# Local attention scores on 168 instead of 192 columns, with a new order of all engines

## The chip, the cores and the metric

The kernel runs on one core of a Trainium2 chip. The metric is the device time of one execution in microseconds (us); lower is better. Three runs of the kernel before took 410.26, 410.98 and 411.16 us, so the median is 410.98 us.

## The reference

The reference is a local-global attention followed by a gated MLP with spatial mixing. All inputs are float32. There are 4 batches, 8 heads, 768 positions and a head dimension of 64. Eight keys (`n_global`) are visible to every query, and a query sees the 96 positions up to its own (`n_local`).

```python
scores = scale * np.matmul(q, k.transpose(0, 1, 3, 2))
is_global = pos[None, :] < int(n_global)
is_local = (rel >= 0) & (rel < int(n_local))
keep = is_global | is_local
dist = np.where(is_global & ~is_local, float(n_local), np.abs(rel))
scores = np.where(keep, scores - slopes * dist, -1e9)
a = softmax(scores)
x = np.matmul(a, v)                       # heads side by side: 768 x 512 per batch
h = gelu(x @ w_in); u, v = halves of h    # 512 columns each
v_n = (v - mean) / sqrt(var + 1e-6) * g_ln
v_s = w_sg @ v_n + b_sg                   # over the 768 positions
out = x + (u * v_s) @ w_out
```

## The kernel before

The attention works in 48 units. A unit is one batch, one pair of heads (four pairs) and one of three thirds of the sequence, that is 256 queries in two tiles of 128 (`units`, line 984 and after). The unit with `u == 0` has the first tile of the sequence, whose 128 queries see only the tile's own 128 keys; every other tile is worked on in halves of 64 queries (`HQ`).

**Key columns of a half.** For 64 queries, `W` = 192 score columns are computed: 96 keys shared by both halves of the tile, and a second block of 96 that differs. `NG` = 32 places at the head of each second block hold the first 32 keys of the sequence, as places for global keys, and 64 hold local keys (`tile_keys`, `unit_keys`, `window`). A unit's keys and its 256 queries come as one load, `qk` (`load_qk`, L1073).

**A unit's steps.** `score` (L1102) issues 8 products of 64 x 64 weights in the four quarters of TensorE's array. In the trace each product is two loads of weights and two matmuls, so a unit shows 16 of each. `softmax` then runs per tile and head, four times per unit: VectorE adds the bias to the scores, scales and takes the row's extreme in one instruction (L1124, which a second record, the read of the accumulator, follows); ScalarE takes the exponential with the row sum (L1129); after one reciprocal per unit, GpSimd (L1149), ScalarE or VectorE multiplies by it. The result `p` is 128 x 2 x 192, taken as three 128 x 128 blocks and transposed. For the first 16 units TensorE transposes (L1210, copied to `pt` at L1215 or L1216). For the other 32, VectorE transposes blocks of 32 x 32 (L1178), four DMAs bring them to DRAM (`far`, L1186) and one brings them back as `pt` (L1190). `weigh` (L1237) then multiplies by `v` in quarters; from unit 20 on, two units go together.

**The MLP.** Its products split every float32 operand into a high and a low part and use three matmuls for each (L589, L590, L591; for the last batch's seven-product scheme L837). They fill TensorE between the attention's products, while batch b + 1's attention runs beside batch b's MLP. GpSimd and VectorE share the splits (L625, L759, L940).

**The order of the work.** The kernel builds a list of operations and a planner (`Plan.order`) places them on PE, ACT, DVE, POOL and the DMA queue of SP, by costs written into the file, by the places of each buffer kind (`PLACES`), and by a due time for each operation that is shifted by a number from the string `SHIFTS`, two characters per operation. Each engine's instructions are emitted in the planned order. Where the planner sees a long idle time of TensorE in the first 29 us it emits products of zeros (L538).

```python
SHIFTS = ( ... )           # two characters per operation: the shift of its due time
NG = 32
W = P + HQ                 # 192
NS = P - NG                # 96
KW = 6 * NS                # 576 key columns of a unit's load
```

`find_general` (L1476 and after) sends the kernel to a slow general path if `n_global` is above `NG` or `n_local` above 97.

Of the kernel before, what the change touches and what calls it, by code (L numbers as in the profile page):

```python
# [19 lines left out]
P = 128  # L20
# [8 lines left out]
NG = 32  # L29
# [7 lines left out]
W = P + HQ  # L37
NS = P - NG
KW = 6 * NS
# [12 lines left out]
    "U5NqP9XReIUIO2NiTdTqScajVZRSS7WOSISDSvSuX5RhRpLyXIPtXbTIUCUWMGTyMkYsTRT3dZU8PLX8SgX8RuXjTlUjUIZrUyUa"  # L52
    "QBNEVEUCaoV0TfOfNOVMUdMTP4KWhrUSUXSmUHScPlTRY0TPW3SkSCSjSeQGQhLJSmQTaeRMPqRRXCS5UFT6VVSTN7SLSPSsObTa"
    "PuV8Q2M7SpPRUnQzT9SVUDVaTcSlVWR0bMURVcUCNkVNWBWlUlPqPaXVQXRtQ5VSUAS5TWQqS4T2NhPsU0ZpRaRbQJNEROOYVoVB"
    "URMtU2UgWDRFSWRDPLRoUCTiTmSXMsV7SuRfVZOxayScT5TwX5PSPxPAc7UrUJT1cZHSOsUWX2W5QOTVY8UJVJUORISfPrX5WaV3"
    "SGNuSKYgNcP9RJJYVWPAVcSiX1STOWT0UCgoj2ajYER0RmXaS8VpOUVJUAUQO0OnaPSdbkJzLfWKLAQmWOUqSSQtQ2QLelQjU5WP"
    "VnMdd5R4QCXMQrWzO7WaMiRuGfOFrNPzWFGWRMVRRaErcvXuRxbEPZK5OsWlazP5deQlbwLcSyVkfLRaOkXCS0S3cVRagNMuZ5ck"
    "XeZfV1coWPVguuQ7U6W3S1NdU2HjWgWmRSLnLFRDPJU9RBPsVlULWgQrUqQqPJShP0KOYMKDjzXMdrJrT0YQMXWoTHSOcYSWNaFZ"
    "SfQzSjQ5WdSOZVRxQ6NrWXRXaEOySUIdQif4OZEVLvYLI47eXbRiSuSqckTpcNVBUAkbTeNDT9Y2VuTQTgUFWLYjRkZfUUTpUMQ1"
    "PLQ2XbSUOhM589UaembHVtWXUoMyUobgaaQnJCTDUWSUN6WoV2UNM8aXXEPKRgFATsQvJDQRWeXTTIOOe6YkDSNDZnMdW5acSIal"  # L60
    "aJXHR7WMV1SaUSbqN7SpQmHxXdOUcoRWLZWCXAg5cfNYHBLQggQ0Z5VtT4jgSyTRPmYAPJSoMDPHZIaNCgLlHHP0OnW2LzhJHzKZ"
    "crMNU5ZILILMWoVxVDOPMRTMOlWNKRHLQ0SaLPTbN357TOOpiQNrPiEOUeaFU5RhLEMWOsPxVKcUVsUmROGRRfaIbQQga8GZGKVW"
    "WPUgaQYvWybiOjVZJBMITeJMHkcHTMRBM8XKJdQrQWXMWVWkPMX5LpLhbJN3TtTdRiWlWvKIQzW8OaV9SdTYNFXCVAL2TXSfe3RD"
    "QtYMTqVJVbTSOoIwWPOxOoTPcGfgZvO3e5NcSwXMThRfUrV3WITIQqTJTtMdWaT3TvWzYXPeXWNBT4SIWgKVa9Q8UkXUUCQdKwWJ"
    "TkVQTWSXOXStW8NSPOYUQlQyTtRdK8ZHcMWVXzYkT8D0YiUZPVQ4TnS4TBX1KDJRWTTHO1PRlxTZXPNmTRQLSlLCYPXnXbRlRsWc"
    "OpT1XhUDV9YrTiRoKkTgLXQZSAMvVCW4TFYCMpJnYd6eVVNLXzPUQKOMQ4VKOkQnSGTdhjX9XbS2Z5Z4NyUlUxPINvThORdHOSV6"
    "R7VMTBPjSNXARHcpS2UzX7R9PNKUVvHQNuQCUiSLQHccTSQwfMSKaOKcSqYbVJNpVNPvRmTzXeU9PIKXRsQDc6XeX5kEWBIjRDRn"
    "OpFvI2QWTCRJQaTmg4VsUFFyZ9VjPeQtP8QsWDTtPnMLSORQQDZJS5RyS5OZXNe4NWR9PATNXSR2cbPLKkLLUrT4XqPuOiNdSjUK"
    "TUTIQMgWa0PXV9ZsS0T9LlQIOaVnTERDd2LdU2WUR9ULQYQQfgbENGWdWsPTNjXZYXQ9ddQlMVS4QIS2OTUkVBN4buZsRBNrTJXe"
    "SBPqZFXOWfMhKkaoXfUscoSMTfUOUMVCT5KgXzUyZuPSdnOVSBW2KmYzRBEcV8STIaU4SuYpTrSrZKSLX0OpMsQoUyMsRLIjIrQT"  # L70
    "TaK4OUa0IxXTb5L9Y3T7PwORWvT7aaTTUuUpUwS6Q5U5OjXHW7M5QCRsRYUZIuSTZqRVVnP6YiXEYbZCRvYwWaOYLeTUe2WyUsWY"
    "ZTNPTLbESWQKRAXlQEUeaaR7WMfOUba4c0OpQnYYaWSwNYPVTLUzWWOnVMa5V5PMO8OTVVKrRkRXJcRWRlRhRnRlkVW9QaQLLjRl"
    "QYUEFhMngZT0dzSzTiQYRoLaOhRDUPUyPAW8VfXIUhS4Sia8NJTyVPTeUDc8SLQVMpfnPGR3RAH2RnR9SEXpdISdQ6QGSnSvT8NL"
    "XLRMFHPCaSY0NXfccAPRWSQBT5ToJsaHV6PBitVUOnIwSvYBSBepS9RuMQSRXALAhWaWUHVpMoV4iqNWTSUUSXWPUyVXb3o6SqOb"
    "WeF3RKXjY8S8W2W8UMM7SqTkT5TuP0WrUgSTO6dHq9jhNaQTXEVCQ1cwUeS5SiVCRYNpX7WrWLWbUJTMWRLgedLmMtZva4MJNrOA"
    "Qud3QFSrN3OyTuEulRSMWiWgQKiTXyWPN5SJb9TXakTfVNRhWITfQpXbQoSZQJTAMmVXeLTQbCkWR0RESBfRTCSvRaUVVRSgS6Sg"
    "C5eJdAPQYaS0TCRUYiHQH0drNoa5PMRPPkPBTvT0YyShS3eMThOeTlFGTOWNaCWKe9RsTmTDZ5YeUmKqQHVCTTOWRkXYTnUhZIVc"
    "JRRyWoYLWhQ1P3TLPQTshXSxUJSYSuVJUjY5UMUXiqVLWWXnVbOtc3Q7H0bRhAKxRsAJTlSb7VQ6XhOXWddmTfDALHYmSJSiVSTH"
    "WAa4LydoSqObD9SrW0WlUobSLaInUhWhWbSOfYW0UFQGIYXVbsTQW3bcbWNJVdCnUePDMeJgP8RDClU1UEMrPGguiSEeSUT1ZoPs"
    "awRpTxSBKSW7PKTLV4XnXYPsWLNjQMWqEkJyY0SAWdWqknUaTth9SpK4VZYRZFH2aZVA8NSPXeLPTfRkLZRuR2b0OqYxUSNYHuT8"  # L80
    "OWdNMAUPRHHqTIShFARyZ6XKULTvS7RjL0UGg3QzQIQ7ZjXHTcQSkhRYS3HIRlU9WzQsTPQq7MTdW9ZEVwcYLDa9SOTyTLHXSQNP"
    "LMS3YgQAaOSfSYM5TyRvcgc7ZyGsezRjanQbQxKeYVY0SgMJFXWESpJqSAO0YCSHNYS5iENxVeKwNmQ3GyPRQKf2UELMSebFVcTa"
    "OJOVSoJkLBa4VkUnU0NmU2POV4O6HNdOL8FkYAYrPbYOV8QoFMH6RwSiesaQWYM3NtNeEqNLORNoX7MoRHXufWZoUbelauVeF1LR"
# [43 lines left out]
def unit_widths(u):  # L127

    return (2 * NS + P, P + VT) if u == 0 else (KW, 2 * VT)


def tile_keys(t):

    first = list(range(NG))
    return (list(range(t - NG, t + HQ)), first + list(range(t - 3 * NG, t - NG)),
            first + list(range(t + HQ, t + P)))


def unit_keys(u):

    t = 2 * u * P
    if u == 0:
        near, _, after = tile_keys(P)
        return near + list(range(P)) + after
    return sum((keys for i in range(2) for keys in tile_keys(t + i * P)), [])
# [3 lines left out]

REST = P + NS  # L150


def window(u, i, e):

    if u == 0:
        return P, P + (NS, NS + P)[e]
    return 3 * NS * i, 3 * NS * i + NS * (1 + e)

# [787 lines left out]
def local_global_attention_moe(tc, qk_in, v_in, q_t, k_t, v_n, n_gl, w_in, g_ln, w_sg_t, b_sg,  # L946
# [33 lines left out]

    units = [(b, j, u) for b in range(B) for u in range(NU) for j in range(NPAIR)]
# [17 lines left out]
    for p0, shared, other in ((0, NG, 3 * NG), (HQ, 3 * NG, 0)):  # L999
        ps = slice(p0, p0 + HQ)  # L1000
        iota(rel[ps, 0:NS], shared, -1, 1)
        iota(rel[ps, NS:P], S, 0, 0)
        iota(rel[ps, P:W], other, -1, 1)

    nc.gpsimd.memset(key, FAR)
    iota(key[:, NS:P], 0, 1, 0)
    iota(rel[:, W:W + P], 0, -1, 1)
    iota(key[:, W:W + NG], 0, 1, 0)
    shared_keys = key[:, NS:NS + 2 * NS].rearrange("p (a k) -> p a k", k=NS)[:, :, 0:NG]

    ident = cp.tile([P, P], F32, name="ident")
    nc.gpsimd.memset(ident, 0.0)
# [476 lines left out]
    def tile_of(kind, i, shape, dtype, name):  # L1489
        return pools.get(kind, ap).tile(shape, dtype, tag=f"{kind}{i}", name=name)  # L1490
# [220 lines left out]
```

## Time and profile before

| what | before |
|---|---|
| median of three runs | 410.98 us |
| span of the profiled execution | 409.3 us |
| busy, share of the span: PE | 397.3 us, 97% |
| DVE | 310.6 us, 76% |
| POOL | 245.5 us, 60% |
| ACT | 231.7 us, 57% |
| chain that ended last | PE 77%, ACT 6%, DVE 6%, DMA 4%, POOL 2% |
| granted TensorE clock, mean | 0.997 |

The span runs from the first to the last instruction of the profiled execution. The profile gives no total time for that execution beside its span; the median of the runs is 1.7 us above the span. PE is TensorE's matmuls, PEld its loads of weights, DVE VectorE, ACT ScalarE, POOL GpSimd and SP SyncE, which here issues the DMAs. The ends of matmuls are modelled, so what one block of products costs is read from the starts: from its first start to the first start of what follows.

### The profile page before, as it was taken

How to read it: one execution, taken by the hardware profiler on the slowest of the kernel's cores; microseconds unless marked ns; L12 is line 12 of the kernel's file. 1: busy time of each engine (PE TensorE's matmuls, PEld its weight loads, DVE VectorE, ACT ScalarE, POOL GpSimd, SP SyncE). 2: the span in 40 equal slices, each digit the busy share in tenths (PEclk: the TensorE clock that was granted, in tenths of full speed). 3: DMA queues.
4: the chain of work that ended last, by engine and by line, in shares of the span. 5: the costliest groups of instructions: out<-in, count | busy, mean ns of one | idle time of the engine just before them, and what ended most of it. 6: DMA issues, size and time to landing. Idle time of an engine off the chain costs nothing.

```text
span 409.3 us, 11232 instructions
## 1 busy us (share of the span) xinstructions
PE 397.3 (97%) x3953; PEld 358.9 (88%) x3953; DVE 310.6 (76%) x1025; ACT 231.7 (57%) x756; POOL 245.5 (60%) x397
## 2 busy tenths in 40 slices
PE   7989999899999999999999999999999999999994
PEld 3768778899988888899999888999999888999994
DVE  6897899999877798976756799957657668823773
ACT  5899999785647656553245566644255243532420
POOL 3776776484769567485354447445354243899870
PEclk9999999999999999999999999999999999999998
DMA  7966766338787767776687684736676621000004
GB/s 215 301 229 190 216 218 197 82 118 270 214 291 232 239 206 204 229 190 212 180 257 240 192 251 126 236 82 196 183 238 176 184 55 40 0 2 0 2 19 143
DMA packets 50367, 70.15 MB, mean 171 GB/s; under 512 B 5888, under 2 KB 34432, under 8 KB 50304
## 3 DMA queue, kind: packets, MB, share of 16 engines
q1 hardware_dynamic: 50304, 69.36, 55.9%
q8 instruction: 33, 0.54, 0.6%
q14 instruction: 30, 0.25, 0.2%
HBM read 50.99 MB, written 18.35 MB: 169 GB/s over the span
## 4 chain that ended last, share of the span: by engine, by line
PE 77%; ACT 6%; DVE 6%; DMA 4%; POOL 2%; SPq 1%; issue 1%; DVEq 0%; POOLq 0%
PE mm_ps L589 21%; PE mm_ps L591 20%; PE mm_ps L590 20%; PE av L1237 6%; PE s_ps L1102 6%; PE mm_ps L837 4%; ACT p L1129 3%; DMA pt<-far 2%; DMA qk<-in_qk_in_dram 1%; ACT pt L1215 1%; POOL p L1149 1%; DVE p L1124 1%; DVE stage L933 1%; DVE stage L935 1%; PE tps L1210 1%
## 5 line engine op out<-in xcount | busy, mean ns | idle before, releaser
L1129 ACT ACTIVATE p<-p,pst 128x192 f32<-128x192 f32 (+1 forms) x192 | 84.2, 442 | 33.8 <-DVE pst L1124 33.2
L1149 POOL TENSOR_SCALAR p<-p,pst 128x192 f32<-128x192 f32 (+1 forms) x182 | 86.3, 491 | 25.6 <-DVE pst L1142 22.7
L591 PE MATMUL mm_ps<-wsg,z 128*128 128x384 f32 x192 | 64.4, 335 | 1.0 <-POOL z L625 1.0
L589 PE MATMUL mm_ps<-wsg,z 128*128 128x384 f32 x192 | 64.6, 337 | 0.0
L590 PE MATMUL mm_ps<-wsg,z 128*128 128x384 f32 x192 | 64.1, 334 | 0.0
L1124 DVE CUSTOM_DVE_ANT_0 p<-s_ps,bias 128x192 f32<-128x192 f32 (+1 forms) x192 | 56.8, 337 | 4.3 <-PE s_ps L1102 3.2
L1237 PEld LDWEIGHTS av<-pt,v 64*64 64x64 f32 x1408 | 41.9, 133 | 10.7 <-ACT pt L1215 3.5
L1237 PE MATMUL av<-pt,v 64*64 64x128 f32 (+1 forms) x1408 | 49.5, 250 | 1.8 <-DMA pt<-far 0.8
L589 PE MATMUL mm_ps<-x,win 128*128 128x384 f32 x128 | 44.3, 346 | 0.0
L1102 PE MATMUL s_ps<-qk 64*64 64x192 f32 (+1 forms) x768 | 42.1, 320 | 1.8 <-DMA qk<-in_qk_in_dram 1.8
L591 PE MATMUL mm_ps<-x,win 128*128 128x384 f32 x128 | 42.9, 335 | 0.0
L590 PE MATMUL mm_ps<-x,win 128*128 128x384 f32 x128 | 42.8, 334 | 0.0
L589 PE MATMUL mm_ps<-win,x 128*128 128x512 f32 x96 | 39.6, 413 | 0.0
L705 POOL TENSOR_TENSOR o<-o,x 128x384 f32<-128x384 f32 x24 | 24.5, 1021 | 24.2 <-DVE o L703 18.9
L591 PE MATMUL mm_ps<-win,x 128*128 128x512 f32 x96 | 37.7, 393 | 0.0
L590 PE MATMUL mm_ps<-win,x 128*128 128x512 f32 x96 | 37.7, 393 | 0.0
L1178 DVE STREAM_TRANSPOSE tt<-p 128x384 f32<-128x384 f32 (+1 forms) x64 | 33.2, 543 | 5.5 <-POOL p L1149 3.4
L591 PEld LDWEIGHTS mm_ps<-wsg,z 128*128 128x128 f32 x192 | 36.0, 188 | 1.5 <-POOL z L625 1.4
L1129 ACT ACTIVATION_READ_ACCUMULATOR p<-p,pst 128x1 f32 x192 | 36.9, 192 | 0.0
L589 PEld LDWEIGHTS mm_ps<-wsg,z 128*128 128x128 f32 x192 | 36.0, 188 | 0.7 <-issue 0.7
L590 PEld LDWEIGHTS mm_ps<-wsg,z 128*128 128x128 f32 x192 | 36.0, 188 | 0.0
L608 DVE SCALAR_TENSOR_TENSOR u<-u,mm_ps 128x384 f32<-128x384 f32 x32 | 17.4, 542 | 21.5 <-ACT u L606 21.5
(132 smaller groups left out, 926.1 us busy)
## 6 DMA issues: line engine op xcount, KB each, us to landing
qk<-in_qk_in_dram SPq DMA_DIRECT2D x32, 416.0 KB, 4.6
far<-tt SPq DMA_DIRECT2D x96, 96.0 KB, 2.2
pt<-far SPq DMA_DIRECT2D x24, 384.0 KB, 4.1
v<-in_v_in_dram SPq DMA_DIRECT2D x32, 256.0 KB, 3.7
out_dram<-o SPq DMA_DIRECT2D x28, 192.0 KB, 2.6
qk<-in_qk_in_dram SPq DMA_DIRECT2D x15, 288.0 KB, 3.6
v<-in_v_in_dram SPq DMA_DIRECT2D x16, 192.0 KB, 4.0
far<-tt SPq DMA_DIRECT2D x32, 80.0 KB, 2.3
```

The source lines that it names most:

```text
L589: mm(ps.ap, ah, bh, start=(i == 0), stop=False)
L590: mm(ps.ap, ah, bl, start=False, stop=False)
L591: mm(ps.ap, al, bh, start=False, stop=(i == n - 1))
L608: op([on_dve(n) + (lambda: nc.vector.scalar_tensor_tensor(out.ap, out.ap, GELU_C, h.ap, ALU.add, ALU.mult),)], [h], [out])
L705: lo = lambda eng: eng.tensor_tensor(o.ap, o.ap, xm[:, 1, :].bitcast(F32), ALU.add)
L837: mm(ps.ap, pa(h)[:, ms], pb(g), start=(first and k == n == 0), stop=True, skip_group_check=True)
L1102: nc.tensor.matmul(to, qk[rows, qc:qc + HQ], keys, start=True, stop=True)
L1124: nc.vector.tensor_tensor_reduce(out=p[:, g, 0:nk], in0=s_ps[h][:, i * W:i * W + nk], in1=bias[:, 2 * j + h, w0:w0 + nk], op0=ALU.add, op1 ...
L1129: op([on_act(nk, 0.225) + (lambda p=p, g=g, nk=nk, i=i: nc.scalar.activation(p[:, g, 0:nk], p[:, g, 0:nk], AF.Exp, bias=st[:, 0, i, g:g + ...
L1149: op([on_pool_ts(nk, -0.10) + (partial(scaled, lambda o, a, c: nc.gpsimd.tensor_scalar(o, a, c, 1.0, ALU.mult, ALU.mult)),),][:1 if n < TU ...
L1178: nc.vector.transpose(out, src.rearrange("p g (b j) -> p g b j", j=QB))
L1237: nc.tensor.matmul(to, v[rows, vc:vc + D], of, stop=True, skip_group_check=True, **kw)
```

## The change

Only 8 places are kept for global keys. A half of 64 queries gets `W` = 64 + 96 + 8 = 168 score columns in two pieces of 84: one that both halves share (76 near keys and the 8 first keys), and one of its own (64 keys before or after, and the 20 first near keys). The load `qk` is reordered and becomes shorter: 760 columns, not 832, and 552, not 576, where `u == 0`. The bias instruction, the exponential and the multiplication run over 168 columns. The tiles `p` keep their 192 columns per head (`WP`): four fixed tiles are allocated and VectorE sets their columns 168 to 191 to zero once at the start, so transposes, `far`, `pt` and the products of `weigh` keep their sizes. The planner's cost of `score` becomes 0.52 and 0.59 us, and the whole string `SHIFTS` is another one.

```diff
-NG = 32
+NG = 8
...
-W = P + HQ
-NS = P - NG
-KW = 6 * NS
+NEAR = 96
+W = HQ + NEAR + NG
+WP = P + HQ
+PIECE = W // 2
+KW, KW0 = 6 * PIECE, 2 * PIECE + P
...
 SHIFTS = (
...
 def unit_widths(u):
-    return (2 * NS + P, P + VT) if u == 0 else (KW, 2 * VT)
+    return (KW0, P + VT) if u == 0 else (KW, 2 * VT)
...
+def tile_pieces(t):
+    near, before, after = tile_keys(t)
+    n = PIECE - HQ
+    return after + near[:n], before + near[:n], near[n:] + list(range(NG))
...
+    padded = [ap.tile([P, 2, WP], F32, tag=f"p{i}", name="p") for i in range(PLACES["p"])]
+    for t in padded:
+        nc.vector.memset(t[:, :, W:WP], 0.0)
...
-        for c0, c1 in ((REST, kw), (0, REST)) if n == 0 else ((0, kw),):
+        for c0, c1 in ((0, REST), (REST, kw)) if n == 0 else ((0, kw),):
...
-                near, far = window(u, i, e)
-                step = far - near
-                keys = qk[rows, near:near + 2 * step].rearrange("p (b k) -> p b k", k=step)[:, :, 0:NS]
-                to = to[:, i * W:(i + 1) * W].rearrange("p (b k) -> p b k", k=NS)
+                first, step = window(u, i, e)
+                keys = qk[rows, first:first + 2 * step].rearrange("p (b k) -> p b k", k=step)[:, :, 0:PIECE]
+                to = to[:, i * W:(i + 1) * W].rearrange("p (b k) -> p b k", k=PIECE)
...
-        return op([on_pe(0.56 if u == 0 else 0.67, 8, True) + (put,)], [qk], s_ps, after)
+        return op([on_pe(0.52 if u == 0 else 0.59, 8, True) + (put,)], [qk], s_ps, after)
...
-        ps = soft[n] = [attn("p", [P, 2, W]) for _ in range(2)]
+        ps = soft[n] = [Buf(lambda i: padded[i], "p") for _ in range(2)]
...
-                    c = a * (W if ng == 2 else P)
+                    c = a * (WP if ng == 2 else P)
...
-                a = g if u == 0 and i == 0 else (0, 2 - r)[g]
+                a = g if u == 0 and i == 0 else (1 - r, 2)[g]
...
-                            part(m, i, r, h, v0[i] + P + e * D, a0[i] + 1 + r, e * HQ, (e + 1) * HQ,
+                            part(m, i, r, h, v0[i] + P + e * D, a0[i] + r, e * HQ, (e + 1) * HQ,
```

## Rows read from the trace of the kernel before

**Rows 1.** The page's part 1: busy us, share of the span, instructions.

```profile
PE 397.3 (97%) x3953; PEld 358.9 (88%) x3953; DVE 310.6 (76%) x1025; ACT 231.7 (57%) x756; POOL 245.5 (60%) x397
```

**Rows 2.** Windows from 8 to 404 us, all engines: stretch, its length, busy time.

```profile
8.00:29.00 21.00, 19.39 (x308) 14.18 (x309) 18.39 (x74) 19.17 (x74) 15.44 (x27) 1.00 0.84 274
29.00:57.00 28.00, 27.92 (x430) 22.17 (x431) 23.27 (x105) 27.20 (x106) 20.61 (x43) 1.00 0.73 228
57.00:79.00 22.00, 20.96 (x172) 17.82 (x170) 21.72 (x72) 19.36 (x61) 14.16 (x20) 1.00 0.44 134
79.00:108.00 29.00, 28.71 (x266) 27.38 (x266) 28.25 (x86) 19.86 (x63) 18.97 (x29) 1.00 0.63 195
108.00:170.00 62.00, 61.16 (x678) 53.44 (x670) 49.86 (x179) 40.06 (x138) 41.69 (x72) 1.00 0.77 234
170.00:404.00 234.00, 234.00 (x2066) 221.47 (x2066) 163.26 (x485) 101.99 (x306) 132.18 (x193) 1.00 0.48 141
```

**Rows 3.** Waits of PE, whole span: us in total, times, longest.

```profile
PE mm_ps L591 <- POOL z L625: 1.0, 1, 1.0
PE av L1237 <- DMA pt<-far: 0.8, 2, 0.5
PE tps L1210 <- POOL p L1149: 0.6, 2, 0.5
```

**Rows 4.** Timeline of PE, score blocks of both kinds and what follows.

```profile
27.08 0.83 PE L1102 MATMUL s_ps<-qk 64*64 64x192 f32 x16
27.73 0.40 PE L1237 MATMUL av<-pt,v 64*64 64x128 f32 x8
...
227.82 0.73 PE L1102 MATMUL s_ps<-qk 64*64 64x128 f32 x16
228.37 0.62 PE L1237 MATMUL av<-pt,v 64*64 64x128 f32 x16
```

**Rows 5.** Windows of L1102 alone: its matmuls before 29 us.

```profile
0.00:29.00 29.00, 7.20 (x128) 4.45 (x128) 1.00 0.79 249
```

**Rows 6.** Groups by form on DVE and ACT: count, busy us, mean ns, idle before.

```profile
L1124 DVE CUSTOM_DVE_ANT_0 p<-s_ps,bias 128x192 f32<-128x192 f32 x160 | 49.6, 348 | 4.0 <-PE s_ps L1102 3.1 <-PE tps L1210 0.5 <-POOL p L1149 0.4
L1124 DVE CUSTOM_DVE_ANT_0 p<-s_ps,bias 128x128 f32<-128x128 f32 x32 | 8.8, 281 | 0.3 <-PE s_ps L1102 0.2
...
L1129 ACT ACTIVATE p<-p,pst 128x192 f32<-128x192 f32 x160 | 71.6, 451 | 30.4 <-DVE pst L1124 29.9 <-DVE stage L935 0.3
L1129 ACT ACTIVATE p<-p,pst 128x128 f32<-128x128 f32 x32 | 12.7, 399 | 3.4 <-DVE pst L1124 3.3
```

**Rows 7.** Timeline of the start, all engines.

```profile
2.43 0.24 DVE L963 TENSOR_SCALAR setup<-setup 128x320 bf16<-128x320 bf16 x1 [1.24 <-POOL setup L994]
...
4.72 0.43 PEld L1102 LDWEIGHTS s_ps<-qk 64*64 64x64 f32 x16 [0.32 <-DMA qk<-in_qk_in_dram]
...
8.07 0.77 PE L1102 MATMUL s_ps<-qk 64*64 64x128 f32 x16 [1.55 <-DMA qk<-in_qk_in_dram]
```

**Rows 8.** DMA issues by line: count, KB each, median us to landing.

```profile
qk<-in_qk_in_dram SPq DMA_DIRECT2D x32, 416.0 KB, 4.6
...
pt<-far SPq DMA_DIRECT2D x24, 384.0 KB, 4.1
```

**Rows 9.** Timeline of PE: a score block that stands alone.

```profile
130.13 0.78 PE L1102 MATMUL s_ps<-qk 64*64 64x128 f32 x16
130.83 0.50 PE L589 MATMUL mm_ps<-win,x 128*128 128x512 f32 x1
131.17 0.40 PE L590 MATMUL mm_ps<-win,x 128*128 128x512 f32 x1
131.40 0.40 PE L591 MATMUL mm_ps<-win,x 128*128 128x512 f32 x1
```

**Rows 10.** Chain of waits in order of time, a transposed block's return to `weigh`.

```profile
163.59 4.49 DMA pt<-far
...
168.22 0.50 PE av L1237 x10
```

More of the change, by code (lines that the diff above doesn't have):

```diff
@@ L57 @@
[L57 to L71, printed above, removed]
@@ L127, in unit_widths @@
 def unit_widths(u):
-    return (2 * NS + P, P + VT) if u == 0 else (KW, 2 * VT)
+    return (KW0, P + VT) if u == 0 else (KW, 2 * VT)
 def tile_keys(t):
-    first = list(range(NG))
-    return (list(range(t - NG, t + HQ)), first + list(range(t - 3 * NG, t - NG)),
-            first + list(range(t + HQ, t + P)))
+    return (list(range(t - 32, t + HQ)), list(range(t - NEAR, t - 32)),
+            list(range(t + HQ, t + P)))
+def tile_pieces(t):
+    near, before, after = tile_keys(t)
+    n = PIECE - HQ
+    return after + near[:n], before + near[:n], near[n:] + list(range(NG))
 def unit_keys(u):
@@ L142, in unit_keys @@
     if u == 0:
[L143 to L150, printed above, removed]
+        after, _, rest = tile_pieces(P)
+        return after, list(range(P)) + rest
+    return sum((keys for i in range(2) for keys in tile_pieces(t + i * P)), [])
+OWN = PIECE + P
+REST = OWN + P
 def window(u, i, e):
     if u == 0:
-        return P, P + (NS, NS + P)[e]
-    return 3 * NS * i, 3 * NS * i + NS * (1 + e)
+        return ((OWN + 32, P - 32), (0, REST))[e]
+    return 3 * PIECE * i + PIECE * (1 - e), PIECE * (1 + e)
 SYNC = 0.07
@@ L998, in local_global_attention_moe @@
     dist = zp.tile([P, W + P], BF16, tag="gt0", name="dist")
-    for p0, shared, other in ((0, NG, 3 * NG), (HQ, 3 * NG, 0)):
+    for p0, shared, other in ((0, 32, NEAR), (HQ, NEAR, 0)):
         ps = slice(p0, p0 + HQ)
-        iota(rel[ps, 0:NS], shared, -1, 1)
-        iota(rel[ps, NS:P], S, 0, 0)
-        iota(rel[ps, P:W], other, -1, 1)
+        iota(rel[ps, 0:HQ], other, -1, 1)
+        iota(rel[ps, HQ:HQ + NEAR], shared, -1, 1)
+        iota(rel[ps, HQ + NEAR:W], S, 0, 0)
     nc.gpsimd.memset(key, FAR)
-    iota(key[:, NS:P], 0, 1, 0)
+    iota(key[:, W - NG:W], 0, 1, 0)
     iota(rel[:, W:W + P], 0, -1, 1)
     iota(key[:, W:W + NG], 0, 1, 0)
-    shared_keys = key[:, NS:NS + 2 * NS].rearrange("p (a k) -> p a k", k=NS)[:, :, 0:NG]
+    shared_keys = key[:, W - NG:W + NG]
     ident = cp.tile([P, P], F32, name="ident")
@@ L1489, in tile_of @@
     def tile_of(kind, i, shape, dtype, name):
+        if kind == "p":
+            return padded[i].rearrange("p g k -> p (g k)")
         return pools.get(kind, ap).tile(shape, dtype, tag=f"{kind}{i}", name=name)
@@ L1665 @@
         if u == 0:
[L1666 to L1667 removed]
+            qk_in[:, :, u, :, 0:QW + KW0] = np.concatenate(
+                (kp[..., keys[0]], qs[..., :P], kp[..., keys[1]], qs[..., P:]), axis=-1)
         else:
[L1669 removed]
+            qk_in[:, :, u, :, 0:QW + KW] = np.concatenate((kp[..., keys], qs), axis=-1)
         v0 = 0
@@ L1676 @@
             near, before, after = tile_keys(i * P)
-            shared, other = near + list(range(NG)), (before[NG:], after[NG:])
+            other = before, after
             for g in range(2):
                 hd = slice((i + g) % 2 * D, ((i + g) % 2 + 1) * D)
-                rows = shared[HQ * g:] + shared[:HQ * g]
-                v_in[:, :, u, :, v0 + hd.start:v0 + hd.stop] = vp[:, :, rows, hd]
+                for half, rows in enumerate((near[:HQ], near[HQ:] + list(range(NG)))):
+                    r0 = (half + 1 - g) % 2 * HQ
+                    v_in[:, :, u, r0:r0 + len(rows), v0 + hd.start:v0 + hd.stop] = vp[:, :, rows, hd]
             for e in range(2):
```

99 lines of the change are left out of this document (55 added, 44 removed).

## The prediction

> **What bounds the kernel now.** I read the page first: PE is busy for 97% of the span, DVE for 76%, POOL and ACT for about 60% [rows 1]. A share over the whole span hides stages, so the windows came next. From 170 to 404 us PE is busy without a gap, while DVE is busy for 163 of 234 us and ACT for 102 [rows 2]: every microsecond that leaves PE there leaves the end. Between 29 and 108 us PE is almost full too, but a second engine is as full beside it: ACT with 27.2 of 28 us, then DVE with 21.7 of 22 and 28.3 of 29 [rows 2]. There a shorter PE is worth something only if ACT and DVE get shorter with it. From 8 to 29 us PE has 1.6 us of idle time (and products of zeros beside that), and ACT is busy for 19.2 of 21. Adding up the idle time of PE over the six stretches gives 1.61 + 0.08 + 1.04 + 0.29 + 0.84 + 0 = 3.86 us. The waits say whom it waits for: once 1.0 us for a split on POOL, otherwise for `p` and `pt`, the output of the softmax and its way back from DRAM [rows 3]. So the kernel is bound by the amount of work on PE, in an order in which almost nothing is late. What the profile must give is how much work the change takes from PE, and whether a new order can be as tight.
>
> **Scores on PE.** The number of products stays; each has 168 columns to run over in place of 192. Two block lengths are in the trace, read from start to start. With 192 columns for both tiles a block takes 27.73 - 27.08 = 0.65 us; in the `u == 0` units, where the first tile has only 128 columns and the second 192, 228.37 - 227.82 = 0.55 us [rows 4]. So 64 columns less in one of the two tiles save 0.10 us, and 24 less save 0.0375 us. A unit with `u` above 0 gains that twice, 0.075 us; a `u == 0` unit once, since its first tile keeps 128 columns. The 128 matmuls of this line before 29 us are 8 units at 16 each [rows 5], by the order of the list four with `u == 0` and four without. After 29 us come 12 of the first kind and 28 of the second: 12 x 0.0375 + 28 x 0.075 = **2.55 us**. The size is between two measured lengths, so little is guessed. Reading starts to 0.01 us leaves it between 2.3 and 2.8.
>
> **Softmax.** The bias instruction falls from 348 ns at 192 columns to 281 at 128, 1.05 ns per column, so 24 columns are worth 25 ns; the exponential falls from 451 to 399, so 20 ns [rows 6]. Four of each per full unit give 0.10 us on DVE and 0.08 on ACT, half of that with `u == 0`. Each is at least PE's own 0.075 or 0.0375. This is why PE's gain can come through in the stretches where ACT and DVE are full as well: all shrink at the same rate per unit. After 170 us these two only get more slack. POOL's multiplication shrinks too; POOL is full nowhere [rows 2], so it goes in at nothing.
>
> **A rule against the gain on PE.** A score block issues 16 weight loads besides its 16 matmuls, and these take 0.43 us together in a block of the short kind [rows 7]; that is below the 0.55 us that the block takes, and the block did get shorter with its columns, so the loads don't set its length at 168 columns either. The Trainium skill, on the page TensorE: Matmul & The Clock Gate (section Back-to-back issue gap), says that in a stream of load and matmul the spacing is set by both, 81 ns at 128 columns and 131 ns at 512. My estimate from that page is 0.13 ns per column, so 16 x 24 x 0.13 = 0.05 us per full unit in place of 0.075, and a sum of 2.55 us for the whole change in place of 3.4. The two block lengths above give 0.10 us / (8 x 64) = 0.195 ns per column, and the row decides.
>
> **The first 29 us.** Here PE waits for the softmax, and its own gain is hidden. Eight units shorten DVE by 4 x 0.05 + 4 x 0.10 = 0.6 us and ACT by 0.48. I take **0.45 us**, as ACT is nearest to full; bounds 0 (weight staging fills what comes free) and 0.6.
>
> **Loads.** Around 8 us PE waits 1.55 us for a `qk` load [rows 7]. Each `u == 0` load loses 24 columns x 128 x 4 bytes = 12 KB; three of them lie ahead of that point. At the 274 GB/s that moved just after [rows 2], 36 KB are 0.13 us. I take **0.1 us**, bounds 0 and 0.13. Later `qk` loads shrink by 36 of 416 KB [rows 8], under a DMA that is no bound; nothing for them, and nothing lost either, for the number of DMAs on SP's queue doesn't change.
>
> **Setting the padding to zero.** Four instructions of 48 elements per partition go onto DVE at the start. DVE stands idle there for 1.24 us until POOL has finished its index rows, and an instruction over 320 columns takes 0.24 us [rows 7]; four of them would be 0.96 us, still under that cover. Zero; without the cover at most 0.96 us of a later bias. `p`, its transposes, `far`, `pt` and the products with `v` keep their sizes: zero. The path test still holds, since eight global keys fit in 8 places; if it failed, the slow path would run and the time would be of another order, which I exclude.
>
> **The new order.** The planner's string is replaced as a whole, and nothing in the trace of before shows an order that doesn't exist yet. Bounds: at best it removes the 3.86 us of idle time and rejoins score blocks that stand alone in the MLP. One such block costs 130.83 - 130.13 = 0.70 us in place of 0.55, and the matmul after it 0.34 in place of 0.23 [rows 9], so 0.26 us; I count four of these (at 130, 142, 155 and 180 us) and two lone parts of `weigh` (at 321 and 333 us), 1.5 us at that price. So -5.4 us at most. On the other side, an order less lucky on the chip than in the plan adds waits like those of before: the same 3.86 us once more doubles them. I take the value nearest to the rows, an order as tight as this one, and with it a small part of the waits: those for `p` and `pt` are 1.4 us in four waits [rows 3], and each has a softmax before it that is about 0.2 us shorter. I put in **0.3 us**, bounds -5.4 and +3.9.
>
> **Sum.** 2.55 + 0.45 + 0.1 + 0.3 = 3.4 us. Against the profiled execution: a span of 409.3 - 3.4 = 405.9 us. The median of the runs stands 1.7 us above that span, and what lies around the span is not changed, so **407.6 us**.
>
> **Rivals.** *A, the new order also tightens.* Half of the 3.86 us idle and of the 1.5 us of lone blocks goes, 2.7 us: 404.9 us. For it: shorter softmaxes on all engines give the planner more slack everywhere before 170 us. Against it: after 170 us, 234 us have no gap to win. Chance 0.21.
>
> *B, the weight loads bound the short score blocks.* Then part of the column gain stays on PE; with the page's rate the sum was 2.55 us and the time 408.4 us. The 0.55 us block speaks against it. Chance 0.04.
>
> *C, nothing left.* The columns go as forecast, but the new order pays it back in new gaps of PE, about 3.4 us in all, nearly as much as the order of before has: 411.0 us. Chance 0.10.
>
> *D, slower, by the way through DRAM.* From unit 16 on, a transposed block comes back to PE by DMA. At 163.6 us such a return of 4.49 us ends just as `weigh` needs it [rows 10], and the two waits for `pt` of before are 0.8 us in all [rows 3]: the margin is thin where an order is pressed. The gaps between these products are filled with MLP products whose number is fixed; a faster PE reaches `weigh` sooner. I count 12 groups of `weigh` after 167 us. If each waited 0.45 us, 5.4 us would be added and 413.0 us would come out; it is slower than before as soon as a group waits over 3.4 / 12 + 0.07 = 0.35 us, the 0.07 being the 0.2% bound. Against it: PE loses only 0.15 us per pair of units, about as much as the softmax before the return gets shorter, and before this wait hardly came after 170 us. Chance 0.09.
>
> **How the numbers follow.** The forecast has 0.56. A measurement of this kernel can tell about 0.2%, 0.8 us, from no change. The forecast, A and B are faster: 0.56 + 0.21 + 0.04 = 0.81; C is no change, 0.10; D slower, 0.09. The range goes from 404.0 us, which holds most of A, to 410.6 us, which holds the bounds of the known terms and the lower part of C. Left out are D, half of C and the far end of A.
>
> **What would show it.** Score blocks from start to start of 0.575 and 0.51 us; bias instructions of about 323 ns and exponentials of about 431 ns at 168 columns; a DVE memset inside an idle stretch before 2.5 us; PE's idle time between 8 us and the last product near 4 us; no gap after 170 us, with the last product some 3.4 us earlier. I am wrong if score blocks keep 0.65 us (B), if PE's idle time after 8 us is below 2 us (A) or over 6.5 us (C), or if the waits for `pt` reach 4 us (D).

## The result and the profile after

The changed kernel took 408.08 us (median of four runs, 406.55 to 408.85), the kernel before 411.07 us in the same rounds. The ratio is 0.9916 with a 95% interval of 0.989 to 0.9943: faster by 0.6 to 1.1%. The forecast was 407.6 us, in a range of 404.0 to 410.6.

The page's part 1 of the changed kernel, and its windows as in [rows 2]:

```profile
PE 395.3 (97%) x3980; PEld 358.5 (88%) x3980; DVE 312.0 (77%) x1041; ACT 226.1 (56%) x746; POOL 233.2 (57%) x395
```

```profile
8.00:29.00 21.00, 19.64 (x334) 15.55 (x323) 18.82 (x79) 20.24 (x80) 14.30 (x28) 1.00 0.78 261
29.00:57.00 28.00, 27.87 (x433) 21.12 (x434) 23.59 (x112) 27.05 (x103) 22.55 (x49) 1.00 0.74 232
57.00:79.00 22.00, 21.81 (x210) 18.37 (x211) 21.67 (x69) 20.96 (x69) 15.35 (x23) 1.00 0.39 116
79.00:108.00 29.00, 29.00 (x238) 28.16 (x237) 28.12 (x89) 18.18 (x60) 18.60 (x27) 1.00 0.63 188
108.00:170.00 62.00, 59.67 (x667) 52.15 (x666) 51.67 (x184) 36.21 (x128) 38.02 (x68) 1.00 0.82 246
```

The 97% of PE is the same as before, and so is the picture behind it: full stretches, here with 1.36 + 0.13 + 0.19 + 0 + 2.33 = 4.0 us of idle time up to 170 us and no wait of PE behind that. What moved is where it idles. Three more profiled executions of the changed kernel, used below, have 3.1, 1.9 and 2.1 us there, so this figure alone says little about the order. The single wait of 1.04 us at 79 us is gone, and between 108 and 170 us there are 2.33 us in place of 0.84.

Who PE waited for, in the changed kernel (us in total, times, longest), as in [rows 3]:

```profile
PE s_ps L1112 <- DMA qk<-in_qk_in_dram: 2.0, 2, 1.2
PE s_ps L547 <- DVE bsg L982: 1.2, 1, 1.2
PE av L1247 <- DVE pst L1152: 1.1, 1, 1.1
PE tps L1220 <- POOL p L1159: 0.7, 2, 0.4
PE av L1247 <- ACT pt L1225: 0.6, 2, 0.3
```

The third line names VectorE, but the wait ends 0.13 us after an instruction that has nothing to do with `weigh`; in a second execution, shown further down, the same place waits for the DMA that brings `pt` back, and here that DMA lands 0.14 us before the wait ends. The first line holds 1.18 us for a `qk` load at 131.4 us. Both are waits for DMAs.

The score blocks of the two kinds in PE's timeline, as in [rows 4], and the groups of the softmax, as in [rows 6]:

```profile
35.08 0.75 PE L1112 MATMUL s_ps<-qk 64*64 64x168 f32 x16
35.65 0.40 PE L1247 MATMUL av<-pt,v 64*64 64x128 f32 x8
...
225.61 0.69 PE L1112 MATMUL s_ps<-qk 64*64 64x128 f32 x16
226.11 0.62 PE L1247 MATMUL av<-pt,v 64*64 64x128 f32 x16
```

```profile
L1134 DVE CUSTOM_DVE_ANT_0 p<-s_ps,bias 128x168 f32<-128x168 f32 x160 | 46.1, 324 | 5.0 <-PE s_ps L1112 3.1 <-issue 1.2 <-PE tps L1220 0.3
...
L1139 ACT ACTIVATE p<-p,pst 128x168 f32<-128x168 f32 x160 | 68.9, 434 | 33.2 <-DVE pst L1134 31.2 <-PE av L1247 1.5
```

A full block takes 35.65 - 35.08 = 0.57 us and a `u == 0` block 0.50 us, so 0.08 and 0.05 us less than before (forecast 0.575 and 0.51). Starts are printed to 0.01 us; other `u == 0` blocks take 0.51 us, and below they are counted with 0.04 us, half of a full block's gain, since one of their two tiles got shorter. The bias instruction takes 324 ns (323 forecast), the exponential 434 (431). VectorE zeroes the padding inside its idle stretch at the start, here in its timeline:

```profile
1.14 0.27 DVE L992 MEMSET p<- 128x48 f32 x4
2.38 0.24 DVE L972 TENSOR_SCALAR setup<-setup 128x296 bf16<-128x296 bf16 x1 [0.96 <-POOL setup L1007]
```

The four of them take 0.27 us together, and VectorE still waits 0.96 us for POOL behind them.

The profiled execution was the slowest of its four runs, with a span of 407.1 us, 2.2 us shorter than before. PE's last group of products starts at 399.10 us, 2.8 us earlier than before (401.89). The rest of the difference lies after it: from there to the end of the span, where the last outputs land, it took 7.4 us before and 8.0 us after, and between 6.9 and 8.2 us in the experiments. A single span is therefore good to about a microsecond. So below, verdicts go by the ratios of all runs, and the place of a gain by the starts of the same block on PE in two traces. A difference of two ratios has an error of its own: with the intervals given, about 1.2 to 1.5 us.

### The profile page after: what moved, and what is told of

Its sections match the earlier page's. It is cut to its first block, busy times and chain, and to the rows that moved or that the text cites. A ratio compares the mean times of both kernels' runs of the same rounds, so it can differ in the third digit from the quotient of the medians.

```text
span 407.1 us, 11302 instructions
## 1 busy us (share of the span) xinstructions
PE 395.3 (97%) x3980; PEld 358.5 (88%) x3980; DVE 312.0 (77%) x1041; ACT 226.1 (56%) x746; POOL 233.2 (57%) x395
## 4 chain that ended last, share of the span: by engine, by line
PE 80%; DVE 8%; DMA 5%; SPq 2%; POOL 1%; issue 1%; ACT 0%; DVEq 0%; ACTq 0%
PE mm_ps L598 21%; PE mm_ps L600 20%; PE mm_ps L599 20%; PE av L1247 7%; PE s_ps L1112 6%; PE mm_ps L846 4%; PE tps L1220 3%; DMA qk<-in_qk_in_dram 3%; DMA far<-tt 2%; SPq L1196 1%; DVE p L1134 1%; POOL p L1159 1%; DMA v<-in_v_in_dram 1%; DVE tt L1188 1%; DVE win L949 1%
## 5 line engine op out<-in xcount | busy, mean ns | idle before, releaser
L1139 ACT ACTIVATE p<-p,pst 128x168 f32<-128x168 f32 (+1 forms) x192 | 81.2, 429 | 34.6 <-DVE pst L1134 32.6
L1159 POOL TENSOR_SCALAR p<-p,pst 128x168 f32<-128x168 f32 (+1 forms) x187 | 84.5, 469 | 24.0 <-DVE pst L1152 22.3
L1134 DVE CUSTOM_DVE_ANT_0 p<-s_ps,bias 128x168 f32<-128x168 f32 (+1 forms) x192 | 53.1, 317 | 6.0 <-PE s_ps L1112 4.0
L1247 PEld LDWEIGHTS av<-pt,v 64*64 64x64 f32 x1408 | 40.6, 133 | 10.6 <-issue 3.8
L1112 PE MATMUL s_ps<-qk 64*64 64x168 f32 (+1 forms) x768 | 38.7, 307 | 2.0 <-DMA qk<-in_qk_in_dram 2.0
L1148 POOL TENSOR_SCALAR pst<-pst 128x4 f32<-128x4 f32 x38 | 9.9, 260 | 46.5 <-ACT p L1139 43.3
```

Of the source, the lines that this page charges most:

```text
L1112: nc.tensor.matmul(to, qk[rows, qc:qc + HQ], keys, start=True, stop=True)
L1134: nc.vector.tensor_tensor_reduce(out=p[:, g, 0:nk], in0=s_ps[h][:, i * W:i * W + nk], in1=bias[:, 2 * j + h, w0:w0 + nk], op0=ALU.add, op1 ...
L1139: op([on_act(nk, 0.225) + (lambda p=p, g=g, nk=nk, i=i: nc.scalar.activation(p[:, g, 0:nk], p[:, g, 0:nk], AF.Exp, bias=st[:, 0, i, g:g + ...
L1159: op([on_pool_ts(nk, -0.10) + (partial(scaled, lambda o, a, c: nc.gpsimd.tensor_scalar(o, a, c, 1.0, ALU.mult, ALU.mult)),),][:1 if n < TU ...
L1247: nc.tensor.matmul(to, v[rows, vc:vc + D], of, stop=True, skip_group_check=True, **kw)
```

## The experiments

The theory to be tested, W: the gain is the work taken from PE, whatever the order. Against it stood O, that the new order makes the gain; S, that the shorter softmax makes it and PE has room; and P, that the new order gives a part back.

### The columns in the old order, and the new order with the old columns

The planner only sees the costs written into the file. If it is told the old costs and the old string, it writes out the old order for the new code, and the other way round.

The first kernel, against the changed one (with the string `SHIFTS` of before):

```diff
+PLANNED = 192
...
-        s_ps = scores[n] = [bank("s_ps", 2 * W) for _ in range(2)]
+        s_ps = scores[n] = [bank("s_ps", 2 * PLANNED) for _ in range(2)]
...
-        return op([on_pe(0.52 if u == 0 else 0.59, 8, True) + (put,)], [qk], s_ps, after)
+        return op([on_pe(0.56 if u == 0 else 0.67, 8, True) + (put,)], [qk], s_ps, after)
...
-                op([on_dve(nk, 0.017)
+                op([on_dve(PLANNED if nk > P else nk, 0.017)
...
```

The other costs (exponential, multiplication, bias tables, size of `qk` loads) are treated alike. The second kernel is the one of before with the new string and `PLANNED = 168`.

> The changed kernel's 168 columns in the order of before: the planner is told the old costs and the old string, so every engine issues its instructions in the order of before. Theory W (the gain is the work taken from TensorE): the columns alone are worth 2.55 to 3.4 us, so 2.5 to 3.5 us below the kernel before, score blocks of 0.57 us, and TensorE's idle time between 8 us and its last product stays at 3 to 4.5 us. Rival O (the new order makes the gain): within 1 us of before.

Measured: 407.5 us against 411.51, ratio 0.9917 (0.9897 to 0.9937), that is 3.4 us, as theory W asked. PE's idle time up to 170 us is 3.0 us.

> The kernel before with 192 columns in the order of the changed kernel (its costs and its string given to the planner, so every engine issues in the new order). Theory W: within 1 us of the kernel before, since the new order is about as tight as the old one. Rival O: about 3 us below before. Third possibility P (the new order loses part of what the columns give): 0.5 to 1.5 us above before, and the kernel of 168 columns in the old order then beats the changed kernel by as much.

Measured: 410.76 us against 411.51, ratio 0.9995 (0.9979 to 1.001).

> The changed kernel once more, on the chip and in the rounds of the other runs, so that it can be set beside them. All theories: 2.4 to 3.5 us below before.

Measured: 407.33 us against 411.51, ratio 0.9909 (0.989 to 0.9929), that is 3.7 us, a little above the expected 3.5.

The columns alone give 0.83%, both together 0.91%, the order alone nothing that can be told from zero. O is out, and P finds no support in the times.

Since two kernels share an order in each pair, the same blocks stand in both traces, and their starts on PE show where the gain is made. The first pair is 192 and 168 columns in the old order, the second the same in the new order (for 168 columns the third of four profiled executions of the changed kernel). Starts in us, from PE's timelines:

```
                       old order: 192   168    gain   new order: 192   168    gain
weigh near 26 us            26.58   25.82   -0.76        27.00   26.16   -0.84
weigh near 57 us            57.54   56.11   -1.43        57.93   56.49   -1.44
transposes near 73 us                                    73.16   71.55   -1.61
products behind them                                     73.41   72.04   -1.37
products near 106 us       106.02  104.30   -1.72
weigh 101 to 106 us        106.64  105.16   -1.48       101.37   99.89   -1.48
weigh near 162 us          167.25  164.54   -2.71       164.04  161.38   -2.66
scores near 178 us         180.00  176.75   -3.25       179.39  176.65   -2.74
weigh near 315 us          318.76  314.23   -4.53       318.07  313.93   -4.14
```

The lines behind the last two rows of the 168 columns, first in the old order, then in the new one (timelines of PE):

```profile
176.75 0.80 PE L1113 MATMUL s_ps<-qk 64*64 64x168 f32 x16
...
314.23 0.45 PE L1249 MATMUL av<-pt,v 64*64 64x128 f32 x8
```

```profile
176.65 0.80 PE L1112 MATMUL s_ps<-qk 64*64 64x168 f32 x16
...
313.93 0.56 PE L1247 MATMUL av<-pt,v 64*64 64x128 f32 x16
```

After 176 us 18 score blocks remain, 4 of them with `u == 0`: 14 x 0.08 + 4 x 0.04 = 1.28 us. The old order shows 4.53 - 3.25 = 1.28, the new one 1.40. Here the gain is PE's own work, within 0.12 us. Up to 57 us both gain more than PE's blocks explain.

From 57 us to the `weigh` at 101 to 106 us the net gain is 0.05 and 0.04 us, although four blocks (0.28 us) lie there. The added rows say where it goes. In the new order the gain has grown to 1.61 us at 73 us, after two blocks; then one start comes back to 1.37. The two lines of the kernel with 192 columns, and those with 168, where the load of the weights waits for VectorE (timelines of PE and PEld):

```profile
73.16 0.49 PE L1212 MATMUL tps<-ident,p 128*128 128x128 f32 x3
73.41 0.42 PE L590 MATMUL mm_ps<-wsg,z 128*128 128x384 f32 x1
```

```profile
71.55 0.49 PE L1220 MATMUL tps<-ident,p 128*128 128x128 f32 x3
72.04 0.45 PE L598 MATMUL mm_ps<-wsg,z 128*128 128x384 f32 x1
...
72.04 0.19 PEld L598 LDWEIGHTS mm_ps<-wsg,z 128*128 128x128 f32 x1 [0.24 <-DVE vg L620]
```

VectorE is busy for 9.08 of the 9.20 us from 62.7 to 71.9 us in that trace, and for only 0.04 us of them with the bias instruction (its window by line):

```profile
62.70:71.90 9.20, 0.04 (x2) 1.00 0.70 220
```

So VectorE had next to nothing there that the change made shorter. Behind 72 us the gain grows again with the next two blocks, from 1.37 to 1.48. In the old order it grows through all four blocks, to 1.72 us, and 0.24 us of it go at one wait for `pt` (timeline of PEld, 168 columns):

```profile
105.16 0.54 PEld L1249 LDWEIGHTS av<-pt,v 64*64 64x64 f32 x24 [0.49 <-DMA pt<-far]
```

Between 106 and 180 us part of the gain is luck of the executions that were profiled: with 192 columns PE waited for `pt`, 0.54 and 0.29 us in the old order and 0.91 us in the new one, and with 168 columns it didn't.

### More work on PE alone

```diff
+SCORED = 240
-                keys = qk[rows, first:first + 2 * step].rearrange("p (b k) -> p b k", k=step)[:, :, 0:PIECE]
-                to = to[:, i * W:(i + 1) * W].rearrange("p (b k) -> p b k", k=PIECE)
+                keys = qk[rows, first:first + SCORED]
+                to = to[:, i * W:i * W + SCORED]
...
```

> The changed kernel in its own order, with the score products run over 240 consecutive columns; the softmax still reads 168. This adds 72 columns on TensorE alone, three times what the change removed (the values of the scores are not the reference's, since the key columns no longer match). Theory W: three times 2.55 us, so 7.6 us above the changed kernel (7 to 9, as blocks before 29 us lose their cover too). Rival S (the shorter softmax makes the gain, TensorE has room): under 2 us above the changed kernel.

Measured: 412.76 us against 411.51, ratio 1.0048 (1.0021 to 1.0076). Against the changed kernel of these rounds that is (1.0048 - 0.9909) x 411.5 = 5.7 us, less than the 7 to 9 expected by W, though by about the error of the difference (1.4 us), and far over S. The blocks grew as they should, here in PE's timeline of this run:

```profile
114.12 0.68 PE L1248 MATMUL av<-pt,v 64*64 64x128 f32 x24
114.62 0.99 PE L1113 MATMUL s_ps<-qk 64*64 64x240 f32 x16
115.43 0.40 PE L1248 MATMUL av<-pt,v 64*64 64x128 f32 x8
...
226.06 0.85 PE L1113 MATMUL s_ps<-qk 64*64 64x128 f32 x16
```

115.43 - 114.62 = 0.81 us, 0.24 more than 0.57, and half of that, 0.12, with `u == 0`. The block at the row of 176.65 us above starts here at 179.17, and the `weigh` at 325.75 us of the changed kernel at 331.91: 2.5 us later in the first half and 3.6 us more in the second. In the second half 14 x 0.24 + 4 x 0.12 = 3.8 us were added, so nearly all comes through. Before it, 22 blocks after 29 us added 14 x 0.24 + 8 x 0.12 = 4.3 us (8 more before that), and only 2.5 came through: a slower PE waits less for others. The same starts say where. From the `weigh` near 57 us to the products behind the wait for VectorE at 72 us the way is 15.00 us long, against 15.55 with 168 columns, although two longer blocks lie in it (57.51 to 72.51 us). From there to the `weigh` near 100 us it is 28.32 against 27.85 us, 0.47 more for two blocks of 0.24: all of it, with VectorE busy for 28.1 of the 29 us from 79 to 108 us. The wait of 1.42 us for a DMA at 120 us that the changed kernel had beside this run is gone.

### One side undone

The same edit with `SCORED = 192` undoes the change on PE alone. The second kernel undoes it on the softmax alone, in the 32 units with `u` above 0:

```diff
-                w0, nk = (W, P) if own else (0, W)
+                w0, nk = (W, P) if own else (0, WP if u else W)
+                c0 = i * W - (WP - W if u and i else 0)
-                    out=p[:, g, 0:nk], in0=s_ps[h][:, i * W:i * W + nk], in1=bias[:, 2 * j + h, w0:w0 + nk],
+                    out=p[:, g, 0:nk], in0=s_ps[h][:, c0:c0 + nk], in1=bias[:, 2 * j + h, w0:w0 + nk],
...
-            nk = P if u == 0 and i == 0 else W
+            nk = P if u == 0 and i == 0 else WP if u else W
```

> The changed kernel in its own order with the score products run over 192 consecutive columns; the softmax still reads 168. This undoes the change on TensorE alone (the scores are not the reference's). Theory W: 1.1 to 2.6 us above the changed kernel of the same rounds: 2.55 us of work, less what TensorE's waits for DMAs of about 1.4 us swallow. Rival S (the shorter softmax makes the gain): under 0.6 us above it.

Measured: 409.02 us against 411.52, ratio 0.9941 (0.9928 to 0.9955).

> The changed kernel in its own order with the bias, the exponential and the multiplication run over 192 columns in the 32 units with u above 0; TensorE's scores keep 168 columns (the softmax takes in 24 columns of the neighbouring tile, so the result is not the reference's). Theory W: 0 to 0.8 us above the changed kernel of the same rounds, from 29 to 108 us, where ACT and DVE are as full as TensorE. Rival S: 2.5 us or more above it.

Measured: 409.56 us against 411.52, ratio 0.9955 (0.9937 to 0.9973).

> The changed kernel beside these runs, on the same chip. All theories: 2.4 to 4 us below before.

Measured: 407.45 us against 411.52, ratio 0.9914 (0.9887 to 0.994).

PE alone is worth (0.9941 - 0.9914) x 411.5 = 1.1 us, the softmax alone 1.7 us, each good to about 1.3 us. The first is at the lower end of W. The second is above the 0.8 us that W allowed and below the 2.5 us that S asked for, though the error reaches both. By the times the two can't be told apart, and the first is not clear of zero. The starts on PE say more. First the changed kernel (its starts at 176.65 and 313.93 us stand above), then PE at 192, then the softmax at 192:

```profile
112.94 0.56 PE L1247 MATMUL av<-pt,v 64*64 64x128 f32 x16
```

```profile
113.15 0.45 PE L1248 MATMUL av<-pt,v 64*64 64x128 f32 x8
...
178.66 0.88 PE L1113 MATMUL s_ps<-qk 64*64 64x192 f32 x16
...
317.06 0.45 PE L1248 MATMUL av<-pt,v 64*64 64x128 f32 x8
```

```profile
113.56 0.56 PE L1249 MATMUL av<-pt,v 64*64 64x128 f32 x15
...
178.38 0.80 PE L1112 MATMUL s_ps<-qk 64*64 64x168 f32 x16
...
315.84 0.56 PE L1249 MATMUL av<-pt,v 64*64 64x128 f32 x16
```

Up to 113 us, PE at 192 costs 0.21 us and the softmax at 192 costs 0.62 us; the two together cost 1.56 us (114.50 us in the kernel with 192 columns in this order, against 112.94). The four executions of the changed kernel are within 0.15 us there (112.79 to 112.94 us). At the `weigh` near 57 us the softmax has already cost 0.59 us, PE 0.03 and both 1.44 (it starts at 56.49 us, and at 57.08, 56.52 and 57.93). From 176 to 314 us it is the reverse: 138.40 us against 137.28 for PE at 192, 1.1 us, and 137.46 for the softmax at 192, 0.2 us, where the four executions of the changed kernel take 137.27 to 137.35. So PE alone sets the time in the second half; in the first 57 us the softmax sets more of it than PE does, and either side alone leaves most of the gain. The middle, 113 to 176 us, adds 1.8 and 1.1 us in these two traces, mostly by one wait for `pt` near 120 us, 1.68 and 1.61 us. The changed kernel has that wait in some executions itself, so this part is not put down to either side. Without it the traces give 1.3 us for PE alone and 0.8 us for the softmax alone.

### The waits for DMAs between 106 and 132 us

Two of the four executions of the changed kernel that were profiled wait for `pt` near 119 us, two don't. Here the DMAs that SP issued in the second of them (its timeline), then PE:

```profile
112.78 0.34 SPq L719 DMA_DIRECT2D out_dram<-o  x1
113.42 0.33 SPq L1086 DMA_DIRECT2D qk<-in_qk_in_dram  x1
114.49 0.33 SPq L1200 DMA_DIRECT2D pt<-far  x1
...
119.66 0.55 PE L1247 MATMUL av<-pt,v 64*64 64x128 f32 x14 [1.42 <-DMA pt<-far]
```

The four beside each other, in us:

```
                                     first   second    third   fourth
weigh near 113 us, PE               112.94   112.92   112.94   112.79
return before, issue to landing        5.8      5.5      4.8      4.3
output issued, SP                   112.83   112.78   111.23   110.58
return issued, SP                   114.55   114.49   112.94   112.28
issue to landing                       4.6      5.0      4.9      5.1
wait for it, PE                       1.06     1.42        0        0
weigh near 315 us, PE               315.97   314.82   313.93   314.10
span                                 407.1    405.1    404.2    404.8
```

The return itself takes about as long in all four. What differs is its issue, 1.6 to 2.3 us later in the first two. In these two SP waited 1.6 us to issue the output ahead of it, by the profile until the return before it had landed:

```profile
SPq L719 <- DMA pt<-far: 1.6, 1, 1.6
```

In the third that wait was 0.5 us, in the fourth there was none. The runs below test another cause, the load between the output and the return.

A `qk` load of 380 KB was issued just ahead of the return. It isn't needed before 125 us, so it was moved behind, in the planned order:

```diff
-        for o in self.search(start):
+        order = self.search(start)
+        for late, behind in ((1024, 934),):
+            late, behind = self.ops[late], self.ops[behind]
+            order.remove(late)
+            order.insert(order.index(behind) + 1, late)
+        for o in order:
```

> The changed kernel with one load moved on SP's queue: the qk load that is issued at 113.4 us goes behind the return of a transposed unit (pt from far) that is issued at 114.5 us and for which TensorE waited 1.4 us at 119.7 us. Theory Q (380 KB of qk ahead of the return make it late): the wait falls under 0.4 us and the kernel is 0.8 to 1.2 us faster than the changed kernel of the same rounds. Rival N (the way itself sets it: its own packets and the issue, or the wait only moves to the moved load): within 0.5 us of the changed kernel, and the wait stays or a wait for qk of about the same length stands a few us later.

Measured: 407.16 us, ratio 0.9911 (0.9888 to 0.9934), beside 0.9914 for the changed kernel. SP's timeline, then PE's:

```profile
114.30 0.33 SPq L1205 DMA_DIRECT2D pt<-far  x1
114.67 0.43 SPq L1091 DMA_DIRECT2D qk<-in_qk_in_dram  x1
...
118.04 0.68 PE L1252 MATMUL av<-pt,v 64*64 64x128 f32 x24
```

Issued at nearly the same time, the return was there for a `weigh` at 118.04 us, with no wait; it took 3.3 us from issue to landing. But PE then waited 0.34 us at 122 us for the split of `w_sg`, whose load landed at 121.55 us, and 0.23 us for a `qk` load at 130 us, and the time is that of the changed kernel. So a second move was added, `((1024, 934), (980, 845))`, which puts that load of `w_sg` ahead of the next four DMAs to `far`.

> The kernel with the qk load behind the return from DRAM, and besides the next load of w_sg ahead of the four DMAs that bring the next transposed unit to DRAM. With the first move alone TensorE no longer waited for the return, but 0.34 us and another 0.4 us at 122 us for a split of w_sg, whose load landed late. Theory Q2 (two late DMAs one behind the other make the rest of the loss at 118 to 131 us): neither wait stands in this trace, and the time is 0.5 to 1.2 us below the changed kernel of the same rounds. Rival N2 (the DMA engines are full from 106 to 132 us, so what is moved ahead makes another thing late): within 0.4 us of the changed kernel, with new waits of TensorE in the same stretch.

Measured: 408.64 us against 411.81, ratio 0.9929 (0.9902 to 0.9956). The return took 4.8 us.

> The kernel with the one qk load behind the return from DRAM, a second time. If the first look was typical: no wait for pt at 118 us, the return lands within 4.2 us of its issue, and the time is within 0.5 us of the changed kernel, since a part of the wait comes back at the split of w_sg. If it was chance, the wait for pt of over 0.8 us is there again.

Measured: 407.79 us, ratio 0.991 (0.9883 to 0.9938). The wait for `pt` near 118 us is 0.23 us, a wait of 0.29 us for the split of `w_sg` follows at 123 us, and a further one of 0.37 us for `pt` stands at 126 us. The return took 4.7 us, not under 4.2 as expected; it was issued 0.8 us earlier than in the first run of this kernel. The ratio is 1.0 us above that of the changed kernel beside it, twice what was expected, but within the error.

> The changed kernel beside these two. All theories: 2.4 to 4 us below before. By the profiles so far TensorE waits for the return from DRAM near 119 us in some executions (1.06 and 1.42 us) and in others not.

Measured: 407.0 us, ratio 0.9885 (0.9863 to 0.9908), with no wait for `pt` near 119 us. That is 4.7 us below before, more than the 4 us expected.

With both moves PE waits again, for `w_sg` and for the next `qk` load (its timeline):

```profile
123.05 0.44 PE L604 MATMUL mm_ps<-wsg,z 128*128 128x384 f32 x1 [0.84 <-DVE wsg L954]
...
131.27 0.45 PE L1117 MATMUL s_ps<-qk 64*64 64x128 f32 x8 [1.09 <-DMA qk<-in_qk_in_dram]
```

No move made the kernel faster. With the load moved behind it the return took 3.3, 4.7 and 4.8 us in three executions, against 4.6 to 5.1 us without the move: only one of them is clearly shorter, and the gain of theory Q did not come. N2 is right about the new waits, but not about the time: with both moves the kernel is (0.9929 - 0.9885) x 411.8 = 1.8 us slower than the changed kernel beside it, and N2 had allowed 0.4. What the window from 106 to 132 us shows of the DMAs agrees with N2. The second number from the end of each line is the mean busy share of the DMA engines: in the old order with 192 columns, in the old order with 168, and in the changed kernel.

```profile
106.00:132.00 26.00, 25.46 (x285) 23.27 (x284) 18.96 (x68) 15.68 (x59) 20.03 (x31) 1.00 0.80 248
```

```profile
106.00:132.00 26.00, 26.00 (x304) 23.69 (x297) 18.77 (x71) 16.96 (x64) 20.39 (x33) 1.00 0.82 249
```

```profile
106.00:132.00 26.00, 23.67 (x276) 21.55 (x274) 19.93 (x76) 16.28 (x61) 17.85 (x31) 1.00 0.93 278
```

The new order puts more transfers into this stretch, and it does so with 192 columns too (0.92). In the new order it is 0.91 to 0.96 in every trace, also in those in which PE hardly waits. With the old place of the load it was the return that came late in some executions, with the moves also `w_sg` and the next `qk`. That a full set of DMA engines is the cause of this is argued, not shown.

## Why the prediction was right

- **The bound.** That PE sets the end was right for the second half: 18 blocks at the forecast sizes are 1.2 us, and 1.28 and 1.40 us were measured. It was too simple for the first 57 us. I had written that ACT and DVE are as full there and shrink with PE; the runs say that there the softmax weighs more than PE.
- **Scores on PE, 2.55 us.** The size per block was right (0.08 measured, 0.075 forecast; `u == 0` 0.04 and 0.0375). By these sizes the term would be about 2.7 us. But undone alone it was worth only 1.1 us in the medians (1.3 us in the traces without the wait near 120 us), since in the first half other waits take up what PE gives back.
- **The rule on weight loads** (the Trainium skill, TensorE: Matmul & The Clock Gate, Back-to-back issue gap) says that load and matmul together set the spacing in such a stream. My estimate from its two figures made a full block 0.05 us shorter, and the sum 2.55 us. The block got 0.08 us shorter, and 0.24 us longer with 72 columns more; the trace doesn't follow that estimate. Rival B falls.
- **The softmax.** Its sizes per instruction were right to 3 ns. The step that failed is "all shrink at the same rate per unit", from which 0.3 us were to come through for the four blocks between 57 and 106 us: net 0.05 and 0.04 came. The blocks did get shorter, and 0.24 us were lost again at a single wait in either order. In the new order it is for VectorE at 72 us, in a piece where VectorE is full with other work than the softmax; in the old one for a return of `pt` at 105 us. Where neither stood in the way, from 72 to 101 us in the new order, the length of PE's blocks came through (0.47 of 0.48 us with 240 columns), with VectorE at 28.1 of 29 us. So it wasn't the busy share that decided.
- **The first 29 us and the loads, 0.45 + 0.1 us.** Measured 0.76 and 0.84 us at the `weigh` near 26 us, so the term was too small by 0.2 to 0.3 us, which about makes up for the stretch from 57 us on. The two parts can't be told apart from these traces: at the score block near 8 us, which waits for a `qk` load, the gain was already 0.60 us in the old order (8.07 to 7.47 us) but 0.14 in the new one (7.93 to 7.78), and the four executions of the changed kernel start that block 0.26 us apart. Up to 57 us the terms (with the blocks from 29 us on) come to 0.45 + 0.1 + 0.41 = 0.96 us, and 1.43 and 1.44 came.
- **The padding, zero.** Right: 0.27 us under an idle time of over a microsecond.
- **The new order, 0.3 us for less waiting.** The order alone measured 0.9995, so zero within 0.2% either way. The idle time of PE up to 170 us was 4.0 us in the first profiled execution, near the 4 us forecast, but 3.1, 1.9 and 2.1 us in the three others; 1.9 is below the 2 us that I had set as a sign of rival A. What differs between them is the waits for DMAs, not the order, and the 2.7 us more that A asked for did not come. Rival C, everything paid back, did not either.
- **Rival D** named the right place and had too high a price: the return of transposed units by DMA is what PE waits for in the new order. It costs up to 1.4 us once in the changed kernel, at one crowded place, and not 0.45 us at each group; after 170 us PE never waited for it.

The sum of 3.4 us stands against 3.0 us between the medians and 3.5 us by the ratio (0.0084 x 411.07); three repeats gave ratios of 0.9909, 0.9914 and 0.9885, 3.5 to 4.7 us. The mechanism, less work on PE, is right where PE is alone. That the sum comes as close as this is in part luck: up to 57 us 0.5 us more came than forecast, from 57 to 106 us 0.2 us less, the 0.3 us for the order are not seen, and the waits for DMAs between 113 and 132 us move a single execution by up to 2 us.

## What to carry to other kernels

Where one engine is full from end to end, price a cut in its work from two lengths that the trace already has, and believe it for the stretches in which that engine is full alone. Where a second engine is as full beside it, its busy share doesn't decide: here the cut was lost at 72 us and came through from there to 101 us, with VectorE full on both sides. Look for the one wait at which the first engine would stand, ask whether what it waits for gets shorter too, and check by comparing the starts of the same instruction in two traces with the same order. When an order is searched anew together with a change, run the change in the old order as well: here it made the whole gain.

## What was not expected

One wait for a DMA, of 1.1 and 1.4 us, is in two executions of the changed kernel and not in two others. The return that PE waits for takes about as long in all four; it is issued later, since SP's queue stood 1.6 us until an earlier return had landed. The four executions are within 0.15 us of each other at 113 us and 2.0 us apart at 315 us, and the way from 176 to 315 us is 137.27 to 137.35 us long in each. So their difference arises between 113 and 176 us, where these waits lie, and one of 1.18 us for a `qk` load at 131 us in the first. Single runs in the first comparison lie up to 2.3 us apart (406.55 to 408.85 us). And a load moved out of the way of the late return went with waits of 0 and 0.23 us in place of 1.42, without making the kernel faster. What makes one return take 5.8 us and another 4.3 us at the same place stays open.
